# Reading the last weight matrix in 22, 5 and 1 rows into one PSUM bank, with the residual put in first and 28 unread products ahead

## The chip, the core and the metric

The kernel runs on one core of one Trainium2 chip. The metric is the device time of one execution in microseconds (us). A core has TensorE (PE, with its weight loads shown as PEld), VectorE (DVE), ScalarE (ACT), GpSimd (POOL) and SyncE (SP), which here issues nearly all DMAs. SBUF is the working memory of 128 partitions; PSUM holds the results of TensorE's products.

## The reference

One decode step for four sequences, batch 4 with one token each, model width 1024. All inputs are bf16.

```python
h  = x + attention(layernorm(x))          # 32 query heads, 4 key/value heads, head size 128
                                          # last 2048 of 8192 cached positions, softmax, @ wo
gate = layernorm(h) @ w1                  # (4, 1024) @ (1024, 3584)
up   = layernorm(h) @ w3                  # (1024, 3584)
out  = h + (silu(gate) * up) @ w2         # (4, 3584) @ (3584, 1024)
```

The weights and the cached keys and values that are needed make up 55.6 MB, and every byte is used once.

## The kernel before

**The ring of weights.** All large inputs go through one SBUF buffer `ring` of 160 KiB a partition. A list `plan` has each transfer's place in the buffer, and `load_next` issues the next one on SyncE's queue. The calls of `load_next` stand between the compute instructions, but what holds a transfer back is that the bytes it overwrites must have been read. The order is wq, keys, values, wo, w1, w3, w2. `w1` lies at 96 to 152 KiB, `w3` at 0 to 56 KiB, `w2` at 56 to 112 KiB, so that w2's later rows overwrite the first rows of w1, and its earlier ones overwrite wo.

**Rows.** A weight matrix lies in SBUF with its input dimension spread over the 128 partitions; a "row" in this text is the slice that each partition holds of one of its input elements. `w2` has `IF` = 28 rows of 1024 elements a partition, 256 KB each. `R1` and `R2` are the row numbers at which pieces of w2 begin; its four pieces have 17, 7, 3 and 1 rows.

**The first half.** Layer norm, the query product (L263), transposes of the keys (L319) that VectorE and ScalarE copy out of PSUM in turn (L323, L325), scores (L304), softmax, the product with the values (L382) and with wo into `y_ps` (L411). `h1` (L424) is the sum with x: 128 partitions, of which four in each group of 32 belong to the four sequences; the 1024 columns are folded into four groups of `CG` = 256.

**The second half.** Four products, one for each group of 32 output partitions, make up one row's work. `gate_up` multiplies w1's eight rows into `g_ps` (two banks) and later w3's into `u_ps` (L459). Inside the w1 part, after its fourth row, `load_next(3)` issues the last three pieces of w2. ScalarE and VectorE make silu of the gate while w3 arrives (L471 to L475), VectorE multiplies it with `u_ps` (L478) and transposes the result into `hgT` (L481).

**The down projection, which changes.** `down` (L492) issues the four products of one row. Rows 0 to 16 go into `y2_ps` with 256 columns each; VectorE then adds `h1` and writes `h2` (L501). Rows 17 to 27 go into two tiles, `ya_ps` and `yb_ps`, each in its own bank, with 128 columns each. After row 23 two fp32 products with an identity matrix (L507) add `h2` to these tiles. At the end VectorE copies `ya_ps` (L513) and ScalarE `yb_ps` (L514) into the two halves of `res`, and ScalarE's queue issues the output DMA (L515).

TensorE takes its products in program order. Semaphores come from a framework that follows which tile each instruction reads and writes; a DMA's completion is waited for by piece.

Of the kernel before, what the change touches and what calls it, by code (L numbers as in the profile page):

```python
# [10 lines left out]
P = 128  # L11
ACT = mybir.ActivationFunctionType
ALU = mybir.AluOpType
AX = mybir.AxisListType
BF16 = mybir.dt.bfloat16
FP32 = mybir.dt.float32
# [3 lines left out]
def kernel(  # L20
# [13 lines left out]
    nc = tc.nc  # L34

    B, _, D = A_x.shape
# [5 lines left out]
    KC = D // P  # L42
# [16 lines left out]
    wide = ctx.enter_context(tc.tile_pool(name="wide", bufs=2))  # L59
# [6 lines left out]
    QD = P // JG  # L66
    RS = QD // B
    CQ = Hq * Dh // JG
    CG = D // JG
# [3 lines left out]
    IF = F // P  # L73
# [4 lines left out]


    RING = 5 * 16384  # L80
    R1, R2 = 17, 24
    RQ = 4
    BS = 2
    wq_v = A_wq.rearrange("(p i) n -> p (i n)", i=KC)
# [3 lines left out]
    w2_v = B_w2.rearrange("(p i) n -> p (i n)", i=IF)  # L88
# [34 lines left out]
    def load_tail(at, src, n, r0, m):  # L123
# [4 lines left out]
    KIB = 512  # L128
# [9 lines left out]
        ("wo", load_rows, (32 * KIB, wo_v, D, 0, 32)),  # L138
        ("w1", load_rows, (96 * KIB, w1_v, N_F, 0, 8)),
        ("w3", load_rows, (0, w3_v, N_F, 0, 8)),  # L140
        ("w2", load_rows, (56 * KIB, w2_v, D, 0, 17)),
        ("w2", load_rows, (90 * KIB, w2_v, D, 17, 7)),
        ("w2", load_rows, (104 * KIB, w2_v, D, 24, 3)),
        ("w2", load_rows, (110 * KIB, w2_v, D, 27, 1)),
    ]
    loaded = {}
    cursor = [0]

    def load_next(n=1):
        for _ in range(n):  # L150
            if cursor[0] < len(plan):
                kind, f, args = plan[cursor[0]]
                loaded.setdefault(kind, []).extend(f(*args))
                cursor[0] += 1
# [13 lines left out]
    for c in range(2):  # L168
        nc.sync.dma_start(
            out=x_q[c * 2 * QD : (c + 1) * 2 * QD : RS, :],  # L170
            in_=x_flat.rearrange("b (j c) -> j b c", j=JG)[2 * c : 2 * c + 2],
# [7 lines left out]
    for c in range(2):  # L179
# [8 lines left out]
        out=xn[:], in0=x_sb[:], scalar1=mv[:, 0:1], scalar2=rstd[:, 0:1],  # L188
# [14 lines left out]
    for r0, ne, ns in SETS:  # L203
# [3 lines left out]
            out=xs[:, len(sl) : len(sl) + ns, : ne * 4].rearrange("b l (i s) -> b l i s", s=4),  # L207
            in_=v[:, KC - 1, :, :, :],
        )
        for l in range(ns):  # L210
            nc.tensor.transpose(
                out=ts_ps[: ne * 4, len(sl), :], in_=xs[:, len(sl), : ne * 4], identity=ident[:B, :B]
# [4 lines left out]
    for _, ne, ns in SETS:  # L217
# [9 lines left out]
    ident_f = const.tile([P, P], FP32)  # L227
    nc.vector.tensor_copy(out=ident_f[:], in_=ident[:])

    perm = const.tile([P, P], BF16)  # L230
    nc.vector.tensor_copy(
        out=perm[:].rearrange("p (h dq) -> p h dq", dq=JG),
        in_=ident[:].rearrange("p (dq h) -> p h dq", dq=JG),
# [12 lines left out]
    for j in range(2, JG):  # L246
        nc.vector.tensor_tensor(
            out=same[:, 0, :], in0=same[:, 0, :], in1=ident[:, j * QD : (j + 1) * QD], op=ALU.add
# [6 lines left out]
    for kc in range(KC):  # L255
        wq_t = loaded["wq"][kc]
        for hf in range(CQ // 512):
            for g in range(JG):
                c0 = g * CQ + hf * 512
                n = min(512, N_Q - CE - c0) if kc == KC - 1 else 512  # L260
                if n <= 0:
# [3 lines left out]
                    lhsT=xnT[:, kc, :],  # L265
                    rhs=wq_t[:, c0 : c0 + n],
                    start=(kc == 0),
                    stop=(kc == KC - 1 or (kc == KC - 2 and c0 + 512 == N_Q)),
                )
        if kc == RQ - 1:  # L270
            load_next()
            for k, np_ in enumerate(sl):
                nc.tensor.matmul(
                    q_ps[QD * (JG - 1) : QD * (JG - 1) + B, CQ - CE : CQ],
                    lhsT=xsT[:np_, k, :],
                    rhs=loaded["side"][k],
                    start=False,
                    stop=False,
# [5 lines left out]
    for r in range(REP):  # L284
        nc.tensor.transpose(out=qt_ps[:, r, :], in_=q_sb[:, r * Dh : (r + 1) * Dh], identity=ident[:])
    nc.vector.tensor_copy(
        out=qz[:, :, : Hkv * QD].rearrange("p b (g z) -> p b g z", g=Hkv)[:, :, :, :REP],
        in_=qt_ps[:].rearrange("p r (g x) -> p x g r", g=Hkv)[:, :B, :, :],
# [24 lines left out]
    for u, (b, n) in enumerate(units):  # L313
        k_v = loaded["k"][b]
        kT = ktpool.tile([P, NJ, P], BF16, tag="kT")
        for t in range(NJ // TB):
            kt_ps = psA.tile([P, TB, P], BF16, tag=f"kt{nt % 4}")
            for jj in range(TB):
                nc.tensor.transpose(  # L319
                    out=kt_ps[:, jj, :], in_=k_v[:, n * NJ + t * TB + jj, :], identity=ident[:]  # L320
# [21 lines left out]
        out=Pm[:], in_=scores_ps[:], func=ACT.Exp, bias=nmax[:], scale=1.0, accum_out=rsum[:]  # L342
# [6 lines left out]
    for c in range(NSB):  # L349
# [4 lines left out]
        for g in range(Hkv):  # L354
            if g % 2 == 0:
                nc.vector.tensor_scalar(  # L356
                    out=z[:, :, g, :], in0=pt_ps[:], scalar1=mask[:, g : g + 1], scalar2=None, op0=ALU.mult
# [10 lines left out]
        out=Dm[:], in0=ident[:].rearrange("p (g b r) -> p b g r", g=Hkv, b=B),  # L368
# [11 lines left out]
    for b in range(B):  # L380
        for j in range(JK):
            nc.tensor.matmul(  # L382
                OT_ps[:, b, :],
                lhsT=loaded["v"][b][:, j, :],
                rhs=PTz[j // NJ][:, (j % NJ) * B + b, :, :],
                start=(j == 0),
                stop=(j == JK - 1),
# [14 lines left out]
    psB = ctx.enter_context(tc.tile_pool(name="psB", bufs=1, space=bass.MemoryType.PSUM))  # L402
    y_ps = psB.tile([P, CG], FP32, tag="y")
    HC = CG // 2
    ya_ps = psB.tile([P, 512], FP32, tag="ya")
    yb_ps = psB.tile([P, 512], FP32, tag="yb")
    g_ps = psB.tile([P, 2, 512], FP32, tag="g")
    u_ps = psB.tile([P, 2, 512], FP32, tag="u")
    for i in range(IO):
        for j in range(JG):  # L410
            nc.tensor.matmul(  # L411
                y_ps[QD * j : QD * (j + 1), :],
                lhsT=o4[:, i, :, :].rearrange("p b s -> p (b s)"),
                rhs=loaded["wo"][i][:, j * CG : (j + 1) * CG],
                start=(i == 0),
                stop=(i == IO - 1),
            )
        if i == 11:
            load_next()
    load_next()  # L420


    h1 = act.tile([P, CG], FP32)
# [20 lines left out]
        out=hn[:], in0=h1[:], scalar1=tot[:, 0:1], scalar2=rstd2[:, 0:1],  # L444
# [5 lines left out]
        out=hnT[:].rearrange("p k x -> p (k x)"), in_=hn[:].rearrange("q (c k) -> q k c", k=KC)  # L450
# [3 lines left out]
    def gate_up(kind, out_ps):  # L454
# [27 lines left out]
        out=hgT[:].rearrange("p i x -> p (i x)"),  # L482
        in_=hg[:].rearrange("q s c -> q (s c)").rearrange("q (c i) -> q i c", i=IF),
# [1 line left out]


    y2_ps = psB.tile([P, CG], FP32, tag="y")
    h2 = wide.tile([P, CG], FP32, tag="w4k")

    def down(i, n, c0, out_ps, **kw):  # L490
        for j in range(JG):
            nc.tensor.matmul(  # L492
                out_ps[QD * j : QD * (j + 1), :n],
                lhsT=hgT[:, i, :],
                rhs=loaded["w2"][i][:, j * CG + c0 : j * CG + c0 + n],
                **kw,
            )

    for i in range(R1):
        down(i, CG, 0, y2_ps, start=(i == 0), stop=(i == R1 - 1))  # L500
    nc.vector.tensor_tensor(out=h2[:], in0=y2_ps[:], in1=h1[:], op=ALU.add)  # L501
    for i in range(R1, IF):
        for c, t in enumerate((ya_ps, yb_ps)):
            down(i, HC, c * HC, t, start=(i == R1), stop=(i == IF - 1), skip_group_check=True)
        if i == R2 - 1:
            for c, t in enumerate((ya_ps, yb_ps)):
                nc.tensor.matmul(  # L507
                    t[:, :HC], lhsT=ident_f[:], rhs=h2[:, c * HC : (c + 1) * HC],
                    start=False, stop=False, skip_group_check=True,
                )  # L510

    res = act.tile([P, CG], BF16)
    nc.vector.tensor_copy(out=res[:, :HC], in_=ya_ps[:, :HC])  # L513
    nc.scalar.copy(out=res[:, HC:], in_=yb_ps[:, :HC])  # L514
    nc.scalar.dma_start(out=out_flat.rearrange("b (j c) -> j b c", j=JG), in_=res[0:P:RS, :])  # L515


# [28 lines left out]
```

## Time and profile before

| | |
|---|---|
| time, median of 3 runs | 137.99 us (137.84 to 138.12) |
| span of the profiled execution, first to last instruction | 136.0 us |
| total of the profiled execution outside its span | not listed apart |
| DMA traffic | 55.75 MB, mean 410 GB/s |
| weight and cache queue, share of 16 engines' span | 95.6% |
| busy: PE / DVE / ACT | 72.3 / 43.9 / 31.0 us |
| mean granted TensorE clock | 0.720 of full speed |

In the profile a line such as `126.06 3.82 PE L492 MATMUL y_ps<-ring,hgT 128*32 128x256 bf16 x68 [4.40 <-DMA ...]` reads: from 126.06 us on, for 3.82 us, TensorE ran 68 products of line 492 into y_ps, with a weight of 128 by 32 and 256 columns; before that it sat idle for 4.40 us, and what ended the idle time was a DMA. The page cuts the span into 40 slices, with a digit for the busy share of each in tenths. The "chain of work that ended last" is followed back from the last instruction, at each step to what released it.

### The profile page before, as it was taken

What the parts mean: (1) busy time and instruction counts of PE and PEld (TensorE: products, weight loads), DVE (VectorE), ACT (ScalarE), POOL (GpSimd) and SP (SyncE); (2) the same over time, 40 slices, a digit from 0 to 9 for tenths busy, and PEclk for the clock granted to TensorE, in tenths of its full rate; (3) what the DMA queues carried; (4) which work ended last, traced back from release to release, by engine and by line L of the source; (5) the groups of instructions that cost most, each with busy time, mean ns of one, the idle gap of its engine ahead of it and who ended that gap; (6) DMA issues with size and microseconds to landing.
All of it is one profiled execution on the core that took longest, in us unless ns stands there. A gap on an engine that the chain in (4) does not pass through costs nothing.

```text
span 136.0 us, 2436 instructions
## 1 busy us (share of the span) xinstructions
PE 72.3 (53%) x1096; PEld 46.1 (34%) x1096; DVE 43.9 (32%) x79; ACT 31.0 (23%) x36; POOL 1.7 (1%) x8
## 2 busy tenths in 40 slices
PE   0004920979898989810525916791097000970981
PEld 0002300268374756500014905570043000430870
DVE  5055000043344444470994001206200596026010
ACT  3000000015555555609294300000001400000000
POOL 5000000000000000000000000000000000000000
PEclk9999975557999999985555555568556855568568
DMA  5999999999999999999989999989989899999970
GB/s 155 464 463 406 412 420 414 429 424 439 424 439 424 424 443 426 410 552 453 463 347 463 463 410 405 477 354 494 439 371 494 371 472 401 399 420 407 424 298 5
DMA packets 2650, 55.75 MB, mean 410 GB/s; under 512 B 296, under 2 KB 464, under 8 KB 720
## 3 DMA queue, kind: packets, MB, share of 16 engines
q1 hardware_dynamic: 2604, 55.58, 95.6%
q8 instruction: 8, 0.13, 0.3%
q10 hardware_dynamic: 36, 0.02, 0.0%
q14 instruction: 2, 0.02, 0.0%
HBM read 55.59 MB, written 0.01 MB: 409 GB/s over the span
## 4 chain that ended last, share of the span: by engine, by line
DMA 54%; PE 25%; ACT 11%; DVE 5%; SPq 2%; issue 1%; ACTq 0%
DMA ring<-in_B_w_dram 38%; DMA ring<-in_A_wq_dram 15%; PE kt_ps L319 11%; ACT kT L325 5%; PE scores_ps L304 5%; ACT z L360 3%; PE q_ps L263 3%; DVE rmax L336 2%; ACT Pm L341 2%; PE OT_ps L382 2%; DVE pT L350 1%; SPq L120 1%; PE g_ps L459 1%; DVE z L356 1%; ACT L341 1%
## 5 line engine op out<-in xcount | busy, mean ns | idle before, releaser
L325 ACT COPY kT<-kt_ps 128x1024 bf16<-128x1024 bf16 x16 | 15.9, 1013 | 13.4 <-PE kt_ps L319 13.4
L319 PE MATMUL kt_ps<-ident,ring 128*128 128x128 bf16 x256 | 18.0, 232 | 0.0
L319 PEld LDWEIGHTS <-ring 128*128 128x128 bf16 x256 | 16.0, 105 | 4.9 <-issue 4.9
L323 DVE COPY kT<-kt_ps 128x1024 bf16<-128x1024 bf16 x16 | 11.1, 692 | 16.5 <-PE kt_ps L319 16.5
L459 PEld LDWEIGHTS <-hnT 128*32 128x32 bf16 x128 | 5.5, 143 | 21.8 <-issue 19.2
L382 PE MATMUL OT_ps<-z,ring 128*128 128x32 bf16 x256 | 7.5, 188 | 8.5 <-ACT z L360 5.0
L459 PE MATMUL u_ps<-ring,hnT 128*32 128x448 bf16 x64 | 6.0, 563 | 11.0 <-DMA ring<-in_B_w_dram 11.0
L304 PE MATMUL scores_ps<-kT,qz 128*32 128x512 bf16 x64 | 9.9, 609 | 2.9 <-ACT kT L325 2.9
L263 PE MATMUL q_ps<-ring,xnT 128*4 128x512 bf16 x63 | 6.7, 595 | 7.8 <-DMA ring<-in_A_wq_dram 7.8
L382 PEld LDWEIGHTS <-ring 128*128 128x128 bf16 x256 | 7.4, 104 | 9.2 <-issue 9.2
L459 PE MATMUL g_ps<-ring,hnT 128*32 128x448 bf16 x64 | 5.9, 558 | 4.9 <-DMA ring<-in_B_w_dram 4.9
L492 PEld LDWEIGHTS <-hgT 128*32 128x32 bf16 x156 | 4.9, 134 | 6.2 <-issue 5.7
L411 PE MATMUL y_ps<-ring,o 128*32 128x256 bf16 x128 | 5.9, 371 | 0.8 <-DVE o L398 0.8
L514 ACT CAST res<-yb_ps 128x128 bf16<-128x128 f32 x1 | 0.3, 266 | 26.1 <-PE yb_ps L492 26.1
L492 PE MATMUL y_ps<-ring,hgT 128*32 128x256 bf16 x68 | 3.8, 419 | 4.4 <-DMA ring<-in_B_w_dram 4.4
L360 ACT ACTIVATE z<-pt_ps,mask 128x512 bf16<-128x512 f32 x8 | 5.3, 687 | 3.5 <-DVE z L356 3.5
L352 PE MATMUL pt_ps<-pT,perm 128*128 128x512 bf16 x4 | 2.4, 607 | 6.8 <-DVE pT L350 6.8
L263 PEld LDWEIGHTS <-xnT 128*4 128x4 bf16 x63 | 2.0, 115 | 11.7 <-issue 11.6
L194 PE MATMUL tp_ps<-ident,xn 4*128 4x4 bf16 x8 | 0.7, 200 | 10.0 <-DVE xn L187 10.0
L356 DVE TENSOR_SCALAR z<-pt_ps,mask 128x512 bf16<-128x512 f32 x8 | 5.5, 741 | 1.2 <-ACT z L360 0.8
L473 DVE RECIPROCAL eg<-eg 128x896 f32<-128x896 f32 x1 | 5.8, 5753 | 0.0
L411 PEld LDWEIGHTS <-o 128*32 128x32 bf16 x128 | 4.4, 131 | 3.1 <-DVE o L398 1.9
(85 smaller groups left out, 50.1 us busy)
## 6 DMA issues: line engine op xcount, KB each, us to landing
ring<-in_B_w_dram SPq DMA_DIRECT2D x2, 7168.0 KB, 22.5
ring<-in_A_k_cache_dram SPq DMA_DIRECT2D x4, 2048.0 KB, 27.6
ring<-in_A_v_cache_dram SPq DMA_DIRECT2D x4, 2048.0 KB, 29.2
ring<-in_B_w_dram SPq DMA_DIRECT2D x1, 4352.0 KB
ring<-in_A_wq_dram SPq DMA_DIRECT2D x1, 4096.0 KB, 12.2
ring<-in_A_wq_dram SPq DMA_DIRECT2D x1, 3968.0 KB
ring<-in_B_w_dram SPq DMA_DIRECT2D x1, 1792.0 KB
ring<-in_B_w_dram SPq DMA_DIRECT2D x1, 768.0 KB
```

The lines of the kernel that those rows point to most:

```text
L263: nc.tensor.matmul(q_ps[QD * g : QD * g + B, hf * 512 : hf * 512 + n], lhsT=xnT[:, kc, :], rhs=wq_t[:, c0 : c0 + n], start=(kc == 0), stop ...
L304: nc.tensor.matmul(scores_ps[QD * g : QD * (g + 1), n * 512 : (n + 1) * 512], lhsT=qz_v[:, z0 : z0 + QD], rhs=kT_v[:, g, :, :], start=(b = ...
L319: nc.tensor.transpose(out=kt_ps[:, jj, :], in_=k_v[:, n * NJ + t * TB + jj, :], identity=ident[:])
L323: nc.vector.tensor_copy(out=kT[:, t * TB : (t + 1) * TB, :], in_=kt_ps[:])
L325: nc.scalar.copy(out=kT[:, t * TB : (t + 1) * TB, :], in_=kt_ps[:])
L356: nc.vector.tensor_scalar(out=z[:, :, g, :], in0=pt_ps[:], scalar1=mask[:, g : g + 1], scalar2=None, op0=ALU.mult)
L360: nc.scalar.mul(out=z[:, :, g, :], in_=pt_ps[:], mul=mask[:, g : g + 1])
L382: nc.tensor.matmul(OT_ps[:, b, :], lhsT=loaded["v"][b][:, j, :], rhs=PTz[j // NJ][:, (j % NJ) * B + b, :, :], start=(j == 0), stop=(j == J ...
L411: nc.tensor.matmul(y_ps[QD * j : QD * (j + 1), :], lhsT=o4[:, i, :, :].rearrange("p b s -> p (b s)"), rhs=loaded["wo"][i][:, j * CG : (j + ...
L459: nc.tensor.matmul(out_ps[QD * j : QD * (j + 1), hf, :HF], lhsT=hnT[:, k, :], rhs=loaded[kind][k][:, c0 : c0 + HF], start=(k == 0), stop=( ...
L473: nc.vector.reciprocal(out=eg[:], in_=eg[:])
L492: nc.tensor.matmul(out_ps[QD * j : QD * (j + 1), :n], lhsT=hgT[:, i, :], rhs=loaded["w2"][i][:, j * CG + c0 : j * CG + c0 + n], **kw,)
```

## The change

The first piece of w2 grows to 22 rows, the second has 5 and the third 1; there are three pieces instead of four. The call of `load_next` after the wo loop is gone, so all three are issued within the w1 products. All 28 rows go into `y2_ps` with 256 columns per product. Ahead of them a fp32 product of the identity with `h1` opens the accumulation in that tile, and 28 products of `perm` (a 128 by 128 bf16 constant) with 512 columns of w3's last row are written to `g_ps`, which nobody reads again. VectorE's add, the identity products in the middle and the tiles `ya_ps`, `yb_ps` and `h2` are gone. The two copies at the end read the two halves of `y2_ps`.

```diff
-    R1, R2 = 17, 24
+    R1, R2 = 22, 27
+    NW = 28
...
-        ("w2", load_rows, (56 * KIB, w2_v, D, 0, 17)),
-        ("w2", load_rows, (90 * KIB, w2_v, D, 17, 7)),
-        ("w2", load_rows, (104 * KIB, w2_v, D, 24, 3)),
-        ("w2", load_rows, (110 * KIB, w2_v, D, 27, 1)),
+        ("w2", load_rows, (56 * KIB, w2_v, D, 0, R1)),
+        ("w2", load_rows, ((56 + 2 * R1) * KIB, w2_v, D, R1, R2 - R1)),
+        ("w2", load_rows, ((56 + 2 * R2) * KIB, w2_v, D, R2, IF - R2)),
...
-    ya_ps = psB.tile([P, 512], FP32, tag="ya")
-    yb_ps = psB.tile([P, 512], FP32, tag="yb")
...
         if i == 11:
             load_next()
-    load_next()
...
     y2_ps = psB.tile([P, CG], FP32, tag="y")
-    h2 = wide.tile([P, CG], FP32, tag="w4k")
-
-    def down(i, n, c0, out_ps, **kw):
+    nc.tensor.matmul(y2_ps[:], lhsT=ident_f[:], rhs=h1[:], start=True, stop=False, skip_group_check=True)
+    for _ in range(NW):
+        nc.tensor.matmul(
+            g_ps[:, 0, :], lhsT=perm[:], rhs=loaded["w3"][KC - 1][:, :512], start=True, stop=True
+        )
+    for i in range(IF):
         for j in range(JG):
             nc.tensor.matmul(
-                out_ps[QD * j : QD * (j + 1), :n],
+                y2_ps[QD * j : QD * (j + 1), :],
                 lhsT=hgT[:, i, :],
-                rhs=loaded["w2"][i][:, j * CG + c0 : j * CG + c0 + n],
-                **kw,
+                rhs=loaded["w2"][i][:, j * CG : (j + 1) * CG],
+                start=False,
+                stop=(i == IF - 1),
+                skip_group_check=True,
             )
 
-    for i in range(R1):
-        down(i, CG, 0, y2_ps, start=(i == 0), stop=(i == R1 - 1))
-    nc.vector.tensor_tensor(out=h2[:], in0=y2_ps[:], in1=h1[:], op=ALU.add)
-    for i in range(R1, IF):
-        for c, t in enumerate((ya_ps, yb_ps)):
-            down(i, HC, c * HC, t, start=(i == R1), stop=(i == IF - 1), skip_group_check=True)
-        if i == R2 - 1:
-            for c, t in enumerate((ya_ps, yb_ps)):
-                nc.tensor.matmul(
-                    t[:, :HC], lhsT=ident_f[:], rhs=h2[:, c * HC : (c + 1) * HC],
-                    start=False, stop=False, skip_group_check=True,
-                )
-
     res = act.tile([P, CG], BF16)
-    nc.vector.tensor_copy(out=res[:, :HC], in_=ya_ps[:, :HC])
-    nc.scalar.copy(out=res[:, HC:], in_=yb_ps[:, :HC])
+    nc.vector.tensor_copy(out=res[:, :HC], in_=y2_ps[:, :HC])
+    nc.scalar.copy(out=res[:, HC:], in_=y2_ps[:, HC:])
```

## The prediction

> **What bounds the kernel now.** I read first the page's slices and its chain of work that ended last, to see which resource owns the span; then the timeline of the last 21 us, where the whole change lies; then busy times by stretch, for TensorE's clock; last, an earlier place where VectorE and ScalarE read one PSUM tile.
>
> The page: the DMA slices and the chain's shares.
>
> ```profile
> DMA  5999999999999999999989999989989899999970
> ...
> DMA 54%; PE 25%; ACT 11%; DVE 5%; SPq 2%; issue 1%; ACTq 0%
> ```
>
> The DMA engines are at 90% or nearly so until the last slice but one. The chain goes through the weight stream, and everything computed late only has to be ready when the next piece lands. The span of 136.0 us is that stream plus what follows its last row.
>
> The timeline of the tail (start us, us, engine, line, operation, count, idle before and who ended it):
>
> ```profile
> 115.70 5.95 PE L459 MATMUL u_ps<-ring,hnT 128*32 128x448 bf16 x64 [11.03 <-DMA ring<-in_B_w_dram]
> ...
> 126.06 3.82 PE L492 MATMUL y_ps<-ring,hgT 128*32 128x256 bf16 x68 [4.40 <-DMA ring<-in_B_w_dram]
> ...
> 130.27 0.30 PE L492 MATMUL ya_ps<-ring,hgT 128*32 128x128 bf16 x4 [0.38 <-DMA ring<-in_B_w_dram]
> ...
> 132.74 0.23 PE L492 MATMUL ya_ps<-ring,hgT 128*32 128x128 bf16 x4
> 132.79 0.23 PE L492 MATMUL yb_ps<-ring,hgT 128*32 128x128 bf16 x4
> 133.02 0.29 DVE L513 CAST res<-ya_ps 128x128 bf16<-128x128 f32 x1 [2.67 <-PE yb_ps L492]
> 133.08 0.27 ACT L514 CAST res<-yb_ps 128x128 bf16<-128x128 f32 x1 [26.10 <-PE yb_ps L492]
> 133.39 0.64 ACTq L515 DMA_DIRECT2D out_dram<-res  x1
> ```
>
> Three things are to be seen. Landings: w3 at 115.70, 17 rows of w2 at 126.06, 7 more at 130.27, that is 4.21/7 = 0.601 us a row (10.36/17 = 0.609 for the first piece). Four rows more put the last at 130.27 + 4 x 0.601 = 132.67, and its products start at 132.74. So TensorE runs within 0.07 us of the stream, and the stream is the bound to the last row. Then the two copies of the result stand side by side, 133.02 to 133.31 on VectorE and 133.08 to 133.35 on ScalarE, from two tiles, and the output DMA goes out at 133.39.
>
> TensorE by stretch (us, busy of PE, PEld, DVE, ACT, POOL, granted clock, DMA share, GB/s); from 117.90 on the stretches are cut where the clock steps:
>
> ```profile
> 32.60:56.40 23.80, 21.47 (x277) 14.23 (x276) 8.99 (x13) 13.87 (x14) 0.00 (x0) 1.00 1.01 429
> 56.46:59.87 3.41, 1.51 (x15) 0.46 (x11) 1.93 (x2) 1.01 (x1) 0.00 (x0) 1.00 1.02 437
> 59.90:63.20 3.30, 0.00 (x0) 0.00 (x0) 1.16 (x2) 2.01 (x2) 0.00 (x0) 0.50 1.37 588
> ...
> 117.90:121.31 3.41, 3.41 (x44) 1.61 (x36) 0.00 (x0) 0.00 (x0) 0.00 (x0) 0.50 0.85 368
> 121.31:124.73 3.42, 0.35 (x8) 0.00 (x0) 2.79 (x2) 0.00 (x0) 0.00 (x0) 1.00 1.04 451
> 124.73:128.14 3.41, 2.08 (x40) 1.82 (x44) 0.00 (x0) 0.00 (x0) 0.00 (x0) 0.50 0.91 389
> 128.14:131.55 3.41, 3.03 (x88) 2.54 (x80) 0.42 (x1) 0.00 (x0) 0.00 (x0) 0.50 0.92 380
> 131.55:134.97 3.42, 1.47 (x52) 1.07 (x43) 0.29 (x1) 0.27 (x1) 0.00 (x0) 1.00 0.14 50
> ```
>
> The clock is 0.50 or 1.00 and changes on a grid of 3.41 us. It rose after windows that were 100% (117.90) and 89% (128.14) busy, not after one of 61% (124.73). It held over 32.60 to 56.40 at 90% busy and fell after windows of 44% (56.46) and 10% (121.31). So nearly all of w2 is multiplied at half clock: 68 products in 3.82 us, 56 ns each, a row 0.225 us. After 131.55 a group of four 128-column products takes 0.055 us, so a row takes 0.11.
>
> And the earlier place where both engines read halves of one PSUM tile, q_ps:
>
> ```profile
> 27.29 0.69 DVE L281 TENSOR_SCALAR q_sb<-q_ps 128x512 bf16<-128x512 f32 x1 [14.77 <-PE q_ps L263]
> 28.01 0.60 ACT L282 ACTIVATE q_sb<-q_ps 128x512 bf16<-128x512 f32 x1 [18.85 <-DVE q_sb L281]
> ```
>
> ScalarE waits there until VectorE has finished, although the columns it reads and writes are others.
>
> **The change, part by part.** Times are on the profiled execution's axis; no total of that execution is listed apart from its span of 136.0. The median of the runs is 137.99, so 1.99 us lies outside the span, and I carry it over unchanged.
>
> *Pieces of 22, 5 and 1 rows.* Bytes and order in the queue stay. The last row still lands at 132.67 to 132.74. One transfer fewer can save something: 0.609 against 0.601 us a row between two piece sizes is 0.008 x 28 = 0.2 us, and I take that as the bound either way, with zero as the value, since both sizes lie within 1.4%. The 22 rows land at 126.06 + 5 x 0.601 = 129.07, the 27th row at 132.08.
>
> *The issue that moves.* The first piece is issued with the others inside the w1 products. It overwrites w1's row 0, so SyncE waits for that row's eight products (98.80 plus two groups of four at 0.37, so 99.6) and issues by 100 (one issue takes 0.33 on the SP queue). w3 fills the stream until 115.70, so w2 is queued some 15 us ahead. Cost nothing; without that cover each us of delay would be a us of span. Behind it on SyncE stand only the other two w2 issues.
>
> *Residual first.* One 128x256 fp32 product opens y2_ps. Two such products of 128 columns take 0.71 us now (131.75 to 132.46, partly warm), so 0.4 to 0.9 us. It runs at 121.65, when u_ps is done and TensorE would be idle. The present four fp32 instructions and VectorE's add (0.42, hidden) vanish; both were already behind the stream. Worth nothing.
>
> *28 unread products.* They start near 122.1 to 122.5 and need only w3's last row and a g_ps that VectorE released at 114.6. By the four-column-group rate, 512 columns warm are 4 x 0.055 = 0.22 us, so 6.2 us; the transposes at L319 (15 in 0.94 us, 63 ns for 128 columns with a full weight load each) give 0.25 us, so 7.0. They end between 128.3 and 129.5. hgT is ready at 124.53 (VectorE's transpose L481, 122.83 + 1.70), so the row products queue behind them in order, but 22 rows aren't there before 129.07. Even an end at 129.5 costs nothing, because the 22 rows warm take 22 x 0.11 = 2.4 us, done by 131.9, and the next piece comes at 132.08. Its five rows take 0.55, to 132.63, and the last row is again taken as it lands. Were the products at half clock throughout, 28 x 0.427 (512 columns at 1.2 per ns, the rate of 128 columns in 0.107) = 12 us would push the end to 134.5 before w2 begins; u_ps has been busy for 5.95 us by then, and a fully busy window of 3.41 us must end by 122.5, so I don't expect it.
>
> So the warm clock removes time that the stream was hiding already: TensorE's whole lag was 0.07 us.
>
> *One bank.* The last row is four products of 256 columns, 0.11 us, like two groups of 128 columns now, so the final product ends at 133.06 as before. But both copies now read y2_ps. By the q_ps rows ScalarE starts when VectorE has finished, 0.03 us later: 133.08 + 0.29 = 133.37, then 133.40 + 0.27 = 133.67, against 133.35. That is +0.32 us, straight on the path to the output DMA. Its bounds are 0 (copies side by side) and 0.35; I take the row's end, since the construction is the same and the z copies from pt_ps (L356, L360) take turns too.
>
> The Trainium skill, page "PSUM — Partial Sum Buffer", section "Terms", says that two engines, readers included, must not be on one bank and quadrant at once. By its letter the wait at q_ps was not needed, the halves being in two banks; yet the row has it. In y2_ps both halves share a bank, so page and row both give the 0.32.
>
> **Sum:** 0.32 for the copies, 0.0 for stream and TensorE, less some hundredths for larger packets: +0.3, a span of 136.3 and a time of 137.99 + 0.3 = 138.3 us.
>
> **Will the clock hold?** Between the unread products' end (128.3) and the landing (129.07) TensorE idles 0.8 us, and again from 131.4 to 132.08. A window that holds one gap is 77% busy, one with both 60 to 70%. The rows bound the drop only between 44% and 90%. If the clock falls at a step during the 22 rows, up to 17 rows cost 0.115 us more each, about 2 us, of which the 0.7 us before the next piece hides a part, and the clock returns within 3.4 us; five rows cold instead of warm add 0.6. I put this case at +0.5 to +1.2 beyond the copies.
>
> The Trainium skill, page "TensorE: Matmul & The Clock Gate", section "Why this matters for your kernels", wants no idle gap above some 3 us between bursts; by it a gap of 0.8 us would never cost the clock, and the time is 138.3. The trace is stricter: the last score product ended at 58.59 and the clock was down from 59.87, 1.3 us later.
>
> **Rivals.** 0.2% (0.28 us) is about what a measurement of this kernel can tell from no change.
>
> 1. *The clock drops between pieces.* Speaks for it: 0.8 us idle and a 44% window that lost the clock. Against: the score phase kept it at 90%. Time 138.3 + 0.5 to 1.2 = 138.8 to 139.5.
> 2. *Not slower: the present kernel pays for a late clock step and the new one doesn't.* Its w2 burst starts at 126.06 and the step came at 131.55; on another position of the grid it comes up to 132.9. Then 7 rows cold (1.5), identity (0.85) and 4 rows (0.9) end near 133.5 against 132.85, about 0.6 us lost. This decides if the step comes after some 132.0, in roughly a quarter of positions. The three runs spread over 0.28 us, so it can't be large in the median. If it is paid half the time it cancels the copies: 138.0, and below 137.7 if the copies also overlap.
> 3. *The unread products overrun.* At half clock throughout, +1.6 for them and 28 rows cold (6.3 us from 134.5 to 140.8): 146. Against: u_ps warms the clock each time.
> 4. *The copies don't take turns.* Then nothing is left on either side: 138.0.
>
> **How the numbers follow.** The copies alone, 138.05 to 138.55: 0.58. Clock drop: 0.20. Overrun: 0.02. Late step: 0.14. Copies side by side: 0.06. The first splits at 138.27 into 0.38 slower and 0.20 same; the second and third are slower; the last two give 0.08 same and 0.12 faster, since where both hold, the new kernel wins by some 0.3. Slower 0.60, same 0.28, faster 0.12. The range leaves out the overrun, the worst clock drops and the largest gain: 137.8 to 139.1; the likeliest case alone has 138.05 to 138.55.
>
> **What would show it.** Right: y2_ps rows from about 129.0 at 0.11 us a row; the last four products within 0.1 us of 132.7; the ScalarE copy waiting for the VectorE copy, starting 0.3 us after it; output DMA 0.3 later than 133.39. Wrong: the copies starting together; rows at 0.225 us after 129; unread products running past 130; a last landing that is off 132.7 by over 0.2 us, which would mean that the pieces matter to the stream.

## The result, and the profile after

The median went from 137.95 us (13 runs, 137.76 to 138.12) to 138.31 us (13 runs, 138.13 to 139.32), +0.36; the ratio is 1.0049 with a 95% interval of 1.0036 to 1.0062. The runs of the changed kernel lie in two groups: eight from 138.13 to 138.33, called the ordinary executions below, and five from 139.00 to 139.32, called the dear ones, with nothing between. The profiled execution took 138.28, of which the span is 136.4 (136.0 before), so it belongs to the first group. The second group is why the ratio is larger than the ratio of the medians, 1.0026.

The tail's timeline after the change, same columns as before:

```profile
115.84 5.67 PE L456 MATMUL u_ps<-ring,hnT 128*32 128x448 bf16 x64 [11.31 <-DMA ring<-in_B_w_dram]
...
121.44 6.22 PE L487 MATMUL g_ps<-ring,perm 128*128 128x512 bf16 x28
...
129.10 2.58 PE L492 MATMUL y_ps<-ring,hgT 128*32 128x256 bf16 x88 [1.45 <-DMA ring<-in_B_w_dram]
...
132.13 0.92 PE L492 MATMUL y_ps<-ring,hgT 128*32 128x256 bf16 x24 [0.45 <-DMA ring<-in_B_w_dram]
...
133.10 0.29 DVE L502 CAST res<-y_ps 128x128 bf16<-128x128 f32 x1 [8.69 <-PE y_ps L492]
133.42 0.27 ACT L503 CAST res<-y_ps 128x128 bf16<-128x128 f32 x1 [26.59 <-DVE res L502]
133.72 0.64 ACTq L504 DMA_DIRECT2D out_dram<-res  x1
```

The 22 rows take 2.58 us where the old kernel's 17 took 3.82, and it is worth nothing: TensorE then waits 0.45 us for the next piece. ScalarE's copy is now released by VectorE's copy, not by TensorE, and the output DMA goes out at 133.72 instead of 133.39. The page's chain has the same shape as before:

```profile
DMA 55%; PE 24%; ACT 11%; DVE 5%; SPq 2%; issue 1%; ACTq 0%
```

By stretch, cut where the clock can step:

```profile
120.87:124.28 3.41, 3.41 (x29) 1.43 (x19) 2.69 (x2) 0.00 (x0) 0.00 (x0) 1.00 0.98 423
124.28:127.70 3.42, 3.38 (x16) 1.44 (x15) 0.13 (x1) 0.00 (x0) 0.00 (x0) 1.00 0.89 386
127.70:131.11 3.41, 2.00 (x76) 2.00 (x79) 0.00 (x0) 0.00 (x0) 0.00 (x0) 1.00 0.87 365
131.11:134.52 3.41, 1.50 (x48) 1.01 (x36) 0.29 (x1) 0.27 (x1) 0.00 (x0) 1.00 0.18 71
```

In this execution the clock is at 1.00 from 120.87 to the end, though the third window is only 59% busy.

### The profile page after: what moved, and what is told of

It reads as the page before. It is cut to its first block, busy times and chain, and to the rows that moved or that the text cites. A ratio compares the mean times of both kernels' runs of the same rounds, so it can differ in the third digit from the quotient of the medians.

```text
span 136.4 us, 2398 instructions
## 1 busy us (share of the span) xinstructions
PE 77.3 (57%) x1078; PEld 46.8 (34%) x1078; DVE 43.6 (32%) x78; ACT 31.0 (23%) x36; POOL 1.7 (1%) x8
## 4 chain that ended last, share of the span: by engine, by line
DMA 55%; PE 24%; ACT 11%; DVE 5%; SPq 2%; issue 1%; ACTq 0%
DMA ring<-in_B_w_dram 40%; DMA ring<-in_A_wq_dram 15%; PE kt_ps L319 10%; ACT kT L325 5%; PE scores_ps L304 5%; ACT z L360 3%; PE q_ps L263 3%; DVE rmax L336 2%; ACT Pm L341 2%; PE OT_ps L382 2%; DVE pT L350 1%; SPq L121 1%; PE g_ps L456 1%; DVE z L356 1%; ACT L341 1%
## 5 line engine op out<-in xcount | busy, mean ns | idle before, releaser
L263 PE MATMUL q_ps<-ring,xnT 128*4 128x512 bf16 x63 | 7.2, 626 | 5.5 <-DMA ring<-in_A_wq_dram 5.5
L487 PE MATMUL g_ps<-ring,perm 128*128 128x512 bf16 x28 | 6.2, 379 | 0.0
L281 DVE TENSOR_SCALAR q_sb<-q_ps 128x512 bf16<-128x512 f32 x1 | 0.7, 692 | 14.6 <-PE q_ps L263 14.6
```

The lines of the kernel that those rows point to most:

```text
L263: nc.tensor.matmul(q_ps[QD * g : QD * g + B, hf * 512 : hf * 512 + n], lhsT=xnT[:, kc, :], rhs=wq_t[:, c0 : c0 + n], start=(kc == 0), stop ...
L487: nc.tensor.matmul(g_ps[:, 0, :], lhsT=perm[:], rhs=loaded["w3"][KC - 1][:, :512], start=True, stop=True)
```

## The experiments

The theory was that the ordinary executions lose their 0.3 us to the two copies taking turns, and the dear ones another 0.8 to a clock that falls while TensorE waits for the 22 rows. The rivals: the pieces or the products cost the 0.3; the dear executions come from the stream.

**Two banks by columns.** All 28 rows in halves into the old tiles `ya_ps` and `yb_ps`, so that the copies read different banks:

```diff
-                y2_ps[QD * j : QD * (j + 1), :],
+                (ya_ps, yb_ps)[c][QD * j : QD * (j + 1), :HC],      # 224 products of 128 columns
...
+    nc.vector.tensor_copy(out=res[:, :HC], in_=ya_ps[:, :HC])
+    nc.scalar.copy(out=res[:, HC:], in_=yb_ps[:, :HC])
```

> The changed kernel, with its 28 rows multiplied in halves of 128 columns into two tiles in banks of their own, so that the two copies at the end read different tiles. Theory (the copies taking turns are the whole 0.3 us of the ordinary executions): VectorE's and ScalarE's copies start within 0.1 us of each other, the ordinary executions fall by 0.3 to about 138.0, level with the kernel before; the dearer executions near 139.1 stay, about 0.3 lower. Rival (the pieces of 22, 5 and 1 rows or TensorE's products cost the 0.3): still 138.2 to 138.3.

Measured: 139.19, four runs between 139.15 and 139.42; ratio 1.0101 (1.0088 to 1.0114). The copies did start side by side (134.23 and 134.29), but the expectation failed: there was no group near 138.0. The profile shows two things. The clock fell at 128.50, after a window that was 35% busy (1.18 of 3.41 us):

```profile
125.09:128.50 3.41, 1.18 (x6) 0.42 (x5) 0.00 (x0) 0.00 (x0) 0.00 (x0) 1.00 0.85 365
128.50:131.91 3.41, 2.97 (x114) 2.97 (x117) 0.00 (x0) 0.00 (x0) 0.00 (x0) 0.50 0.89 367
```

And TensorE stopped for 0.38 us in the middle of a row, with nothing that the profile shows to wait for:

```profile
132.40 0.23 PE L499 MATMUL yb_ps<-ring,hgT 128*32 128x128 bf16 x2
133.01 0.23 PE L499 MATMUL yb_ps<-ring,hgT 128*32 128x128 bf16 x2 [0.38 <-issue]
```

The stop is taken up below.

**One bank in the kernel before.** Rows 17 to 27 in 256 columns into `ya_ps` alone, both copies reading it; nothing else changed.

> The kernel before, with only the tail's two tiles made one: rows 17 to 27 in 256 columns into one bank, and both copies reading it. Theory: the copies take turns, +0.3, about 138.25, and no execution near 139. Rival (the turn costs nothing on the path): 137.95.

Measured: 138.13 against 137.85, ratio 1.0021 (1.0012 to 1.0030), no run above 138.29. Its timeline has the new wait without any of the rest of the change:

```profile
133.04 0.29 DVE L510 CAST res<-ya_ps 128x128 bf16<-128x128 f32 x1 [2.67 <-PE ya_ps L491]
133.36 0.27 ACT L511 CAST res<-ya_ps 128x128 bf16<-128x128 f32 x1 [26.36 <-DVE res L510]
133.66 0.64 ACTq L512 DMA_DIRECT2D out_dram<-res  x1
```

So one shared tile alone costs 0.28 us, with four pieces, cold rows and no unread products. That is nearly the whole of what the ordinary executions lose. Whether the tile or the bank makes the copies take turns is not told apart: wherever the copies at the end take turns they read one tile, and no run was made with two tiles in one bank. The prediction's q_ps row, where the copies took turns on two banks of one tile, speaks for the tile.

**36 unread products** (`NW = 36`):

> The changed kernel with 36 unread products instead of 28, so that they end near 121.44 + 36 x 0.2135 = 129.1, where the 22 rows land, and TensorE's idle 1.45 us before the landing is gone. Theory (the dearer executions near 139.1 are those in which the clock falls after that idle time): all executions at 138.2 to 138.4, none above 138.7. Rival (the dearer executions come from the stream or from elsewhere): still about a third near 139.1.

Measured: 138.15, ten runs from 138.07 to 138.22; ratio 1.0022 (1.0013 to 1.0031). The dear group is gone. TensorE goes from the last unread product into the rows without a wait:

```profile
121.21 7.94 PE L487 MATMUL g_ps<-ring,perm 128*128 128x512 bf16 x36
...
129.09 2.58 PE L492 MATMUL y_ps<-ring,hgT 128*32 128x256 bf16 x88
```

Two later kernels with 36 such products and one tile or two with 112 row products had 12 and 11 runs without a dear one either.

**20 unread products** (`NW = 20`):

> The changed kernel with 20 unread products, which end near 125.7, so that TensorE idles 3.2 us before the landing at 129.1. Theory (clock falls after the idle time): most or all executions are dear, 138.9 to 140.4, with rows at 0.225 us after 129.1 in the profile and a granted clock of 0.50 there. Rival (dearer executions have another cause): the same mix as with 28.

Measured: 138.82, seven runs from 138.04 to 139.12, four of them at 138.8 or above. That is a mix, not the "most or all" that was expected. Its profile is of an ordinary execution with a wait of 2.94 us before the rows, over which the clock held:

```profile
124.74:128.15 3.41, 1.42 (x7) 0.55 (x6) 0.00 (x0) 0.00 (x0) 0.00 (x0) 1.00 0.94 408
128.15:131.57 3.42, 2.47 (x88) 2.39 (x88) 0.00 (x0) 0.00 (x0) 0.00 (x0) 1.00 0.89 371
```

A window that was 42% busy did not cost the clock. So the length of the wait doesn't decide by itself: 2.94 us was harmless here, while 2.67 us (128.94 after 126.27) cost the clock in the first two-bank run, where the wait took more of one window and left it 35% busy.

**The changed kernel again**, to meet a dear execution in the profile:

> The changed kernel again, unchanged, for its two groups of times. Theory (the clock falls in a window that is less than some 40% busy, which happens when an early step has shortened u_ps): about 4 in 10 executions near 139.0, the rest near 138.2, and if the profile is of a dear one, its clock is 0.50 from a step between 128.5 and 130.2 on and its rows take 0.225 us. Rival: a dear execution has its clock at 1.00 and a late landing or a stop.

Measured: three of eight runs at 139.04 to 139.06, five from 138.09 to 138.33; with the first 13 that is 8 dear in 21. The profile is of a dear one, 139.06:

```profile
115.75 4.70 PE L456 MATMUL u_ps<-ring,hnT 128*32 128x448 bf16 x64 [12.28 <-DMA ring<-in_B_w_dram]
...
129.02 4.90 PE L492 MATMUL y_ps<-ring,hgT 128*32 128x256 bf16 x112 [2.42 <-DMA ring<-in_B_w_dram]
...
133.97 0.29 DVE L502 CAST res<-y_ps 128x128 bf16<-128x128 f32 x1 [10.63 <-PE y_ps L492]
```

```profile
118.81:122.22 3.41, 3.36 (x44) 1.63 (x38) 1.69 (x2) 0.00 (x0) 0.00 (x0) 1.00 1.01 436
122.22:125.64 3.42, 3.42 (x18) 1.54 (x16) 1.12 (x1) 0.00 (x0) 0.00 (x0) 1.00 1.00 435
125.64:129.05 3.41, 0.99 (x9) 0.34 (x11) 0.00 (x0) 0.00 (x0) 0.00 (x0) 1.00 0.73 312
129.05:132.46 3.41, 3.41 (x68) 2.87 (x71) 0.00 (x0) 0.00 (x0) 0.00 (x0) 0.50 0.76 313
```

This is the mechanism, step by step. The grid lies so that the clock rises at 118.81 instead of 120.87, so u_ps takes 4.70 us instead of 5.67, and the unread products start and end a us earlier (126.60 against 127.66). The rows still land at 129.02, so the wait grows from 1.45 to 2.42 us. The window that ends at 129.05 was 0.99/3.41 = 29% busy, and the clock falls just as the rows start. They all land in time but take 4.90 us without a pause, and the copy starts at 133.97 instead of 133.10: +0.87. The last byte arrived at the same time in both (132.38 and 132.40 in the trace), so the stream is cleared.

**No unread products** (`NW = 0`):

> The changed kernel without unread products. Theory: w2's 22 rows start at half clock at 129.1 and take 0.225 us each; the clock steps up between 132.1 and 135.5, so the last product ends between 133.7 and 135.4 instead of 132.9; with the copies' turn this is 139.0 to 140.7, spread over that whole range. Rival (the unread products do nothing for the path): 138.1 to 138.3.

Measured: 139.40, six runs from 138.57 to 140.27; ratio 1.0105 (1.0073 to 1.0136). Dear as expected, and as wide, though two runs (138.57 and 138.80) lie below the expected 139.0. That the spread comes from where the clock's step falls among the rows is argued; the one profile, of a run at 139.35, has the step at 133.09. So the products are needed with a 22-row piece, to win back what that piece lost: a cold TensorE takes 22 x 0.225 = 4.95 us for what arrives 3.0 us before the next piece.

**20 unread products in the kernel before**, ahead of its 17 rows:

> The kernel before with 20 unread products ahead of its w2 rows (they end near 126, where its 17 rows land), and nothing else changed. Theory: the rows run at full clock, but each piece is waited for as before, so 137.8 to 137.9, within 0.1 of the kernel before. Rival (the kernel before loses time to the half clock, as the second rival of the prediction has it): 137.5 to 137.7, and a narrower spread.

Measured: 138.04, twelve runs from 137.73 to 138.87; ratio 1.0020 (1.0003 to 1.0036). No gain, so the cold rows weren't what bound the kernel before. But the spread is wider than the theory has it: four runs lie above 138.4. The profile is of a run at 137.75 with the clock at 1.00 throughout the rows, and doesn't show what the four lost; that stays open.

**One copy of 256 columns** on VectorE, with 36 unread products:

> The changed kernel with 36 unread products and a single VectorE copy of all 256 columns of y2_ps instead of the two copies in turn. By the VectorE sum of 256 fp32 columns at L421 (0.42 us) against 0.29 + 0.03 + 0.27 = 0.59, theory: 0.15 below the run with 36 products, 138.0. Rival (the copies are not what ends the span): 138.15.

Measured: 138.21, ratio 1.0027 (1.0018 to 1.0035); no gain. The copy took 0.43 and the output DMA went out at 133.45, 0.24 earlier than with two copies in turn, yet the span is the same 136.4.

```profile
133.00 0.43 DVE L502 CAST res<-y_ps 128x256 bf16<-128x256 f32 x1 [9.36 <-PE y_ps L492]
133.45 0.64 ACTq L503 DMA_DIRECT2D out_dram<-res  x1
```

In the trace ScalarE's closing drain instruction stands at 136.03, when SyncE's is long over (135.69); with two copies both were at 135.91. The semaphore wait ahead of that drain ended 0.22 earlier than with two copies (135.62 against 135.84), but the drain followed it after 0.41 us instead of 0.07. So the gain was lost behind the copies, in ScalarE's last instructions; what held them is open.

**Two banks by columns, and 36 unread products:**

> The changed kernel with 36 unread products and with the rows in halves in two tiles in banks of their own. It has both cures. Theory: copies side by side and the clock held, 137.85, level with the kernel before, no execution above 138.2. Rival (the 224 narrower products cost TensorE time of their own, as a stall of 0.6 us at 132.4 in the first two-bank run's profile may say): 138.2 to 139.2.

Measured: 139.18, four runs from 139.13 to 139.47; ratio 1.0098 (1.0083 to 1.0113). The rival was right. The clock was at 1.00, and TensorE stopped again, for longer:

```profile
131.37 0.22 PE L499 MATMUL yb_ps<-ring,hgT 128*32 128x128 bf16 x2
133.05 0.23 PE L499 MATMUL yb_ps<-ring,hgT 128*32 128x128 bf16 x2 [1.46 <-issue]
```

It stops between the second and third of four products that share a row and a tile, so no landing and no semaphore of the kernel can be the cause. It had done 142 of the 224 row products here and 150 in the first two-bank run, which with 36 and 28 unread ones makes 178 both times. And it went on at 133.05 and 133.01, 2.3 and 2.2 us after a 16 KB packet of the instruction queue started (130.72 and 130.79 in the trace).

**More instructions, one bank.** `NW = 100` with 184 columns each, a TensorE time like that of 36 wide ones:

> One bank as in the changed kernel, but the 36 unread products of 512 columns are replaced by 100 of 184 columns, which take TensorE nearly as long (100 x 0.079 = 7.9 us against 7.7). In both two-bank runs TensorE stopped in the middle of a row after the same number of products, counted from the first unread one: 28 + 150 = 178 and 36 + 142 = 178, and went on at 133.0. Theory (the stop is the load of the next block of TensorE's code, so it hangs on the count of instructions alone): here it comes after 78 of the 112 row products, near 131.3, ends near 133.0, and the time is 138.9 to 139.3. Rival (the stop belongs to the halves and the two tiles): no stop, 138.15 as with 36 products.

Measured: 138.22, eight runs from 138.19 to 138.34; ratio 1.0027 (1.0017 to 1.0037). No stop and no dear run:

```profile
129.66 3.34 PE L492 MATMUL y_ps<-ring,hgT 128*32 128x256 bf16 x112
```

The theory as it was put, that the count of instructions alone decides, fell. But the instruction packet that began at 130.7 in the others began at 127.09 here, so what is loaded had come by the time it was needed. The theory became: TensorE's code comes in blocks of 128 products with their weight loads; a block's load begins a while after the one before it is entered, and is usable some 2.3 us later. A boundary costs time where the block before it was entered less than these two times together earlier. If the block before begins 128 products ahead, at product 50, it was entered at 129.46 and 129.59 in the first and second two-bank runs, so the packet came 1.3 and 1.1 us later, and TensorE went on 3.5 us after the entry in both.

**Two banks by columns, shifted.** The two-bank kernel with the 100 narrow products. Counted from the first unread product the boundaries are then at 178 and 178 + 128 = 306:

> The two-bank kernel (224 row products in halves) with 100 unread products of 184 columns instead of 28 of 512. In the runs with 28 and 36, TensorE stopped after 178 products from the first unread one, and no stop came with 100 narrow products and one bank, where the code transfer before that place began at 127.1 instead of 130.7. Theory (blocks of 128 products; a block's load starts when the block before it is entered, and takes over 2 us to be usable): product 178 is passed without a stop, the next boundary is product 306, after 206 of the 224 row products, its load starts near 131.9, and TensorE stops there until 133.5 to 134.3; time 138.6 to 139.4. Rival (the halves in two tiles stall by themselves): a stop again near the 78th or the 150th row product. Second rival (no stop): 137.95 to 138.05.

Measured: 139.84, four runs from 139.62 to 140.14; ratio 1.0141 (1.0124 to 1.0158). Product 178 is passed without a stop. The stop comes where the theory had put it:

```profile
132.48 0.24 PE L499 MATMUL yb_ps<-ring,hgT 128*32 128x128 bf16 x2
134.71 0.23 PE L499 MATMUL yb_ps<-ring,hgT 128*32 128x128 bf16 x2 [2.00 <-issue]
```

From 129.05 on there are 22 rows of eight, seven groups of four and these two, 176 + 28 + 2 = 206 products, which makes 306 with the 100. The instruction queue's packet began at 132.36, and TensorE went on 2.35 later. The trace's DMA view of 132.3 to 132.5 us has that packet (queue 8, one packet of 0.02 MB):

```profile
q8 instruction: 1, 0.02, 30.0%
```

The stop was longer than expected (to 134.71, not 134.3 at most), and so was the time. Product 178 ran at 130.13, 5.3 us after product 50, and the packet began 2.2 us after it, not 1.1 to 1.3. That the place follows the count is shown; what sets the delay of the packet and what fills the 2.3 us is not.

**Two banks by output partitions.** Groups 0 and 1 into `ya_ps`, 2 and 3 into `yb_ps`, so that the product count stays 112; 36 unread products:

```diff
-                y2_ps[QD * j : QD * (j + 1), :],
+                (ya_ps, yb_ps)[j // 2][QD * j : QD * (j + 1), :],
...
+    nc.vector.tensor_copy(out=res[:HP, :], in_=ya_ps[:HP, :])      # HP = 64
+    nc.scalar.copy(out=res[HP:, :], in_=yb_ps[HP:, :])
```

> 36 unread products, and two tiles in banks of their own split by output partitions instead of columns: groups 0 and 1 go to the first tile, 2 and 3 to the second, 256 columns per product, so the count of products stays 112 and the stop after 178 products isn't reached. VectorE copies partitions 0 to 63, ScalarE 64 to 127. Theory: the copies stand side by side, the longer one takes about 0.43 (as VectorE's single copy of 256 columns) instead of 0.59 in turn, so 0.15 to 0.2 below the run with 36 products: 137.95 to 138.05. Rival (copies in turn aren't what costs 0.3): 138.15.

Measured: 137.97, eleven runs from 137.92 to 138.12; ratio 1.0009 (1.0001 to 1.0018). As expected:

```profile
133.02 0.42 DVE L508 CAST res<-ya_ps 64x256 bf16<-64x256 f32 x1 [9.63 <-PE yb_ps L498]
133.06 0.37 ACT L509 CAST res<-yb_ps 64x256 bf16<-64x256 f32 x1 [27.24 <-PE yb_ps L498]
133.51 0.64 ACTq L510 DMA_DIRECT2D out_dram<-res  x1
```

Against the same kernel with one bank (138.15) it wins back 0.18 of the 0.3, and it is the best of the versions with the new pieces. It doesn't beat the kernel before: a copy of 256 columns is 0.13 longer than one of 128. No run pointed to a version that beats both kernels.

## Why the prediction was right

*The stream as the bound.* Held. The 22 rows landed at 129.10 (129.07 was worked out), the next five at 132.13 (132.08), and the last byte came at 132.39 in the trace before and at 132.40 after. Neither the piece sizes nor the later issue (SyncE issued at 99.91) moved it.

*Warm rows worth nothing on the path.* Held: the 22 rows took 1.2 us less than the old 17, and then TensorE waited. The run with 20 unread products in the kernel before gained nothing either.

*The copies.* The term of +0.32 was right in kind and size: the output DMA went out 0.33 later, and the kernel before with one shared tile measured +0.28 alone.

*The residual first.* Costs nothing, but not where the prediction had it. The framework put it at the earliest place its data allowed, right behind VectorE's h1 and not at 121.65:

```profile
92.26 0.70 PE L485 MATMUL y_ps<-h,ident_f 128*128 128x256 f32 x2 [0.59 <-DVE h L421]
```

*The unread products.* The step that failed is their end. 28 were put at 6.2 to 7.0 us, starting between 122.1 and 122.5. They took 6.22 (eight more add 7.94 - 6.22, so 0.215 each), but they started at 121.44, since the identity was not in front of them, and ended at 127.66. So TensorE's wait was 1.45 us, not 0.8, and 2.42 where the clock rises early, a case that the prediction did not work out at all: an early rise of the clock shortens the cover that is to keep the clock up.

*The clock drop as a rival.* Its price, 0.5 to 1.2 beyond the copies, holds the measured 0.8 (139.06 against 138.27, the medians of the two groups in the first 13 runs). Its chance of 0.20 was too small against 8 in 21. It follows from the wait above: with 0.8 us no window could be 29% busy. By this the forecast of 138.3 came out at the ordinary executions, and the interval of the ratio lies higher than their +0.3 alone.

*The second rival*, that the kernel before pays for a late step, found no support: its cold and warm versions don't differ in the right direction.

The page on TensorE's clock, "TensorE: Matmul & The Clock Gate" of the Trainium skill, allows idle gaps up to some 3 us ("Why this matters for your kernels"). The ordinary profile with 20 products kept its clock over 2.94 us, as the page has it, but the dear profile lost it 2.45 us after the last unread product, and there the measurement stands against the page. In the windows that hold the wait behind the unread products, those left 29% and 35% busy lost the clock and those left 42% and 59% busy kept it. Neither the gap nor the busy share of the window sorts all cases here: the clock held after 42% in the run with 20 products, and fell after 44% in the kernel before (56.46 to 59.87).

## What to carry to other kernels

Where the weight stream bounds the kernel, look for what stands behind the last landing, not for what is faster ahead of it; merging two result tiles into one made two engines' copies take turns and cost 0.3 us, while 1.2 us of TensorE time saved in front of the landing was worth nothing. Filler that is to hold TensorE's clock must reach to the landing in the execution where the clock rises earliest, since there it runs out first; 28 products failed in 8 of 21 runs and 36 in none of 10. And count instructions as well as time: the cure with twice as many half-size products cost more than the fault, while the split by output partitions kept their number and worked.

## What the hardware showed that was not expected

In three kernels TensorE stopped for 0.4 to 2.0 us in the middle of a row, two after 178 products from the first unread one and one after 306, and went on 2.2 to 2.35 us after a 16 KB packet of the instruction queue had started. The Trainium skill's page "Runtime: NRT & Kernel Launch", section "Instruction fetch mechanics", has code come in blocks of 256 instructions, which fits 128 products with 128 weight loads; it also says that crossing a block is mostly hidden, and here it was not. By the theory of these runs that is because the products were short (14 ns each in halves at full clock): a block of 128 lasts 1.8 us at that pace, less than the 2.3 that a load took to be usable, and less than the 3.5 to 4.6 us that passed from entering a block to going on with the next.
